# Chunked attention with a gated MLP on one core: two weight-sum sets a step from block 1, earlier splits at block changes, and P2 ahead of P7 in each first group

## The chip, the core and the metric

The kernel runs on one core of a Trainium2 chip. The core has five instruction queues that run side by side and meet at semaphores: TensorE (PE in the profile; its weight loads, PEld, overlap with its matmuls), VectorE (DVE), ScalarE (ACT), GpSimd (POOL) and SyncE (SP), which here issues all the transfers between memory and the on-chip buffers. Each queue runs its instructions in order, so an instruction that waits holds everything behind it on its own queue. The metric is device microseconds of one execution; three runs of the kernel before gave a median of 950.69 us (950.37 to 951.47).

## The reference, cut to what matters

```python
# q, k, v: (8, 8, 576, 64); attention inside chunks of 64
scores = scale * matmul(q_c, k_c.T); attn = softmax(scores); out = matmul(attn, v_c)
x = out.transpose(0, 2, 1, 3).reshape(4608, 512)
# w_gate, w_val: (512, 1536), w_out: (1536, 512)
gate = 1 / (1 + exp(-(x @ w_gate)));  val = x @ w_val
return (gate * val) @ w_out
```

All of it is float32. The kernel keeps the accuracy by splitting each operand into a high and a low part and adding three products (high by high, low by high, high by low) instead of one.

## The kernel before, in words

The 4608 tokens are nine blocks of 512 (m or n counts them), and the hidden width of 1536 is twelve tiles of 128 (f). Blocks 0 to 2 are computed plainly. A step of such a block is `hidden(m, f)`: 24 matmuls (L261) into two banks g0 (gate) and g1 (value), a sigmoid on ScalarE, a product on VectorE (`hf`, L272), and the split into `hh` and `hl`; then `down` (L287): 12 matmuls that add this tile's share to four accumulators `acc`. `down` runs one step behind `hidden`. After the last tile of a block four output copies (`evacuate`, L305 on ScalarE and L307 on VectorE, two each) empty the accumulators into tiles `ob`, and SP sends them out (L308).

Blocks 3 to 8 are computed as three pairs with a seven-product scheme in place of eight block products. P1 to P7 are `product(n, p, which, r, ...)` at L421: for each of 12 groups (p of six, gate or value), `first` computes P1 into bank x (`cx`) and P6 into y (`cy`), with `s1` and `u2` (L439) taken off them; `middle` computes P5 into z (`cz`), P7 on top of y and P2 on top of x; `last` computes P4 and P3. Then the output products (`outward`, L496) run for the pair's two blocks b = 0 and 1, twelve tiles each, every tile after a `split` into `hh` (ScalarE, L486) and `hl` (VectorE, L488).

The seven products need sums of weight quarters. There are 24 sets of them, and `keep_sums` (L331 to L349) computes one: two sums into a tile `a_val`, four into `a_sum`, then a high and a low part into `a_both`, all on GpSimd, and a transfer of `a_both` to memory by SP (L348). `a_val` and `a_sum` share the two buffers of the tag "ob" with the output copies' `ob` tiles of blocks 0 and 1 (and the first two of block 2), handed out in turn in the order of the program. `a_both` has one buffer. `keep(n)` emits the next n sets; it stands at the end of each step of blocks 1 and 2. GpSimd does nothing else in these blocks and runs through its sets as fast as buffers and `a_both`'s transfers let it, not in step with TensorE. In blocks 1 and 2 the order of TensorE and of VectorE is the program's, written out by hand; SP's order is set when the kernel is built, and is fixed then.

Beside the blocks runs the attention of later blocks, in units of two: SP loads `qt` and `kbd` (L149, L152) for scores, and `vt` (L158) for values; TensorE computes scores `sc` (L170) and values `av` (L231); VectorE does the softmax and its transposes (L520 to L560). `tick(share)` hands out VectorE's part of this work in small pieces at the places where it is called, and `insert` puts `sc` and `av` between other matmuls. `load_group` (L365, L368) brings given quarters and sums of a group back from memory into the buffers of weight tiles that are done with.

Of the kernel before, what the change touches and what calls it, by code (L numbers as in the profile page):

```python
# [19 lines left out]
NF = 12  # L20
# [24 lines left out]
SHARES = {1: 2.5, 2: 2.8, "up": 1.05, "down": 1.3}  # L45
# [3 lines left out]
def chunk_attn_moe(ctx: ExitStack, tc: tile.TileContext, q, k, v, w, out):  # L49
# [270 lines left out]
    def keep_given(p, which):  # L320

        t = given[p, which] = dp.tile([P, 3, 2, 256], F32, name=f"given{p}{which}")
        for n, (f, k) in enumerate(((2 * p, 0), (2 * p, 1), (2 * p + 1, 1))):
            nc.sync.dma_start(t[:, n], wt[f, which][:, :, k * 256:(k + 1) * 256].bitcast(F32))
# [6 lines left out]
    def keep_sums(p, which, c):  # L331

        if c == 0:
            sums[p, which] = dp.tile([P, 4, 2, 256], F32, name=f"sums{p}{which}")
        val = mp.tile([P, 4, P], F32, tag="ob", name="a_val")
        for n in range(2):
            parts = wt[2 * p + n, which].rearrange("p a (k c n) -> p a k c n", k=2, c=2)[:, :, :, c].bitcast(F32)
            nc.gpsimd.tensor_tensor(out=val[:, 2 * n:2 * n + 2], in0=parts[:, 0], in1=parts[:, 1], op=ALU.add)  # L338
        sm4 = mp.tile([P, 4, P], F32, tag="ob", name="a_sum")
        for o, x, y, op in (  # L340
            (sm4[:, 1], val[:, 2], val[:, 3], ALU.add), (sm4[:, 0], sm4[:, 1], val[:, 0], ALU.subtract),
            (sm4[:, 2], val[:, 0], val[:, 2], ALU.subtract), (sm4[:, 3], val[:, 1], sm4[:, 0], ALU.subtract),
        ):
            nc.gpsimd.tensor_tensor(out=o, in0=x, in1=y, op=op)  # L344
        both = wp.tile([P, 4, 2, P], F32R, tag="spare", name="a_both")
        nc.gpsimd.tensor_copy(both[:, :, 0], sm4)  # L346
        nc.gpsimd.tensor_tensor(out=both[:, :, 1], in0=sm4, in1=both[:, :, 0].bitcast(F32), op=ALU.subtract)  # L347
        nc.sync.dma_start(  # L348
            sums[p, which][:, :, c], both.rearrange("p s a n -> p s (a n)").bitcast(F32))  # L349
# [66 lines left out]
    def product(n, p, which, r, bank, start, stop):  # L416
        lhs, name = groups[n, p, which][r]
        x, k = xc[n, name], 0
        for c in range(2):
            for wpart, part in ((0, 0), (0, 1), (1, 0)):  # L420
                nc.tensor.matmul(  # L421
                    bank, lhsT=lhs(wpart, c), rhs=x[:, part, c], start=start and k == 0, stop=stop and k == 5,
                    skip_group_check=True)
                k += 1

    def sole(n, p, which):
        z = ps_g.tile([P, TB], F32, tag=f"g{which}", name="cz", bufs=1)
        product(n, p, which, 5, z, True, True)
        return z
# [12 lines left out]
    def gated(n, f, b, value):  # L442

        h = hid[n, f][:, b]
        nc.vector.tensor_tensor(out=h, in0=value, in1=h, op=ALU.mult)

    def middle(n, p, which):
        x, y, s1, u2 = banks[n, p, which]
        f = 2 * p
        if which == 0:  # L450
            for i in range(2):
                hid[n, f + i] = wp.tile([P, 2, TB], F32, tag=f"o{f + i}", name="hid")
        z = banks.pop((n, "z"), None) or sole(n, p, which)
        product(n, p, which, 7, y, False, True)
        u3 = mp.tile([P, TB], F32, tag="ob", name="u3")
        nc.vector.tensor_tensor(out=u3, in0=y, in1=s1, op=ALU.add)  # L456
        c22 = hid[n, f + 1][:, 1] if which == 0 else u3
        nc.vector.tensor_tensor(out=c22, in0=z, in1=u3, op=ALU.add)
        product(n, p, which, 2, x, False, True)
        if which == 0:  # L460
            nc.scalar.activation(hid[n, f][:, 0], x, AF.Sigmoid)
        else:
            gated(n, f + 1, 1, u3)
            gated(n, f, 0, x)
        banks[n, p, which] = y, z, s1, u2
# [17 lines left out]
    def split(n, f, b):  # L483
        h = hid[n, f][:, b]
        hh = mp.tile([P, TB], F32R, name="hh")
        nc.scalar.copy(hh, h)  # L486
        hl = mp.tile([P, TB], F32R, name="hl")
        nc.vector.tensor_tensor(out=hl, in0=h, in1=hh.bitcast(F32), op=ALU.subtract)  # L488
        return hh, hl
# [75 lines left out]
    def advance():  # L565
        now["unit"] += 2 * (now["item"] == "A")
        now["item"] = next(ahead, None)
        now["since"] = now["ticks"]

    def tick(share):  # L570
        now["ticks"] += 1
        now["credit"] += share
        while now["item"] is not None:
            if isinstance(now["item"], float):
                if now["credit"] < now["item"] / 2:
                    return
                now["credit"] -= now["item"]
            elif not (now["item"] == "wait" and now["ticks"] > now["since"] + 1
                      or now["item"][0] == "open" and now["item"][1] <= now["open"]):
                break  # L580
            advance()
        now["credit"] = min(now["credit"], share)
# [19 lines left out]
    def finish():  # L602
        down(*pending.pop(0))
# [30 lines left out]
    def keep(n):  # L634
        for _ in range(n):
            if kept:
                p, which, c = kept.pop(0)
                if c == 0:
                    keep_given(p, which)
                keep_sums(p, which, c)  # L640

    def rest():
        for m in range(1, FIRST_PAIR):
            upto = 4 * (m + 2) if m == 1 else 4 * (m + 3)
            for f in range(2 if m == 1 else 0, NF):
                if m == 2 and f == 7:
                    now["open"] = 0
                step(m, f, "")
                tick(SHARES[m])
                insert(upto, 2)  # L650
                finish()
                tick(SHARES[m])
                insert(upto, 2)
                if m == 1:
                    keep_outer(f)
                    if f == 11:
                        keep_outer(0), keep_outer(1)
                    keep(1)
                else:
                    keep(2)  # L660
                    if f == 8:
                        for which in range(2):
                            load_group(0, 0, which)
        for n in range(3):
            m0 = FIRST_PAIR + 2 * n
            upto = 4 * (m0 + 4)
            order = [(p, which) for p in range(6) for which in range(2)]
            due(n)
            for i, (p, which) in enumerate(order):
                if i + 1 < len(order) and i > 0:  # L670
                    load_group(n, *order[i + 1])
                if pending:
                    banks[n, "z"] = sole(n, p, which)
                    while pending:
                        finish()
                first(n, p, which)
                tick(SHARES["up"])
                if i:
                    last(n, *order[i - 1])
                    tick(SHARES["up"] if i < 11 else 0)  # L680
                    insert(upto, 1)
                middle(n, p, which)
                tick(SHARES["up"] if i < 11 else 0)
                insert(upto, 1)
            load_outer(0), load_outer(1)
            parts = split(n, 0, 0)
            last(n, *order[-1])
            now["open"] = n + 1
            for b in range(2):
                for f in range(NF):  # L690
                    if f % 2 == 0:
                        later = 6 * b + f // 2 + 2
                        if later < 12:
                            load_outer(later % 6)
                        elif n + 1 < 3:
                            load_group(n + 1, 0, later - 12)
                    hh, hl = parts if (b, f) == (0, 0) else split(n, f, b)
                    tick(SHARES["down"])
                    if (n, b) == (2, 1) and f >= NF - 2:
                        pending.append((f, hh, hl))  # L700
                        continue
                    for t in range(4):
                        outward(m0 + b, f, t, hh, hl)
                    insert(upto, 1)

        for i, tiles in ((0, (0, 1, 2)), (1, (0,)), (0, (3,)), (1, (1, 2, 3))):
            f, hh, hl = pending[i]
            for t in tiles:
                outward(NB - 1, f, t, hh, hl)
# [34 lines left out]
```

## Time and profile before

| | |
|---|---|
| median of three runs | 950.69 us (950.37 to 951.47) |
| the profiled execution: its own time, and its span | 949.0 us, 947.2 us |
| TensorE busy | 927.4 us, 98% of the span |
| VectorE, ScalarE, GpSimd busy | 601.1, 340.5, 139.0 us |
| GpSimd's 24 sets | 149.4 to 209.2 us (ten) and 265.1 to 353.1 us (fourteen) |
| block 1's output copies | 259.0 to 263.4 us |
| first group of the seven-product part | from 364.6 us |

The span is from the first to the last instruction; some 2 us of a run lie around it. A row of the timeline has the start in us, the duration in us (several instructions merged where it says x2 or more), engine, line, operation and tiles, and in brackets how long the engine had stood idle before it and what released it. A row of the waits has who waited for whom, the time in total, the number of times and the longest, in us. "SPq" is a transfer being issued.

### The profile page before, as it was taken

To read this page: it belongs to the slowest core of one execution; us is meant where nothing else is said; L and a number is where in the kernel's file an instruction comes from. 1 tells how busy PE (TensorE), PEld (TensorE's weight loads), DVE (VectorE), ACT (ScalarE), POOL (GpSimd) and SP (SyncE) were. 2 spreads that over 40 slices of the span, in tenths; PEclk is the share of its full clock that TensorE was granted. 3 is DMA by queue.
4 is the path that set the end of the run, shared out by engine and by line. 5 is a ranking of instruction groups with operands and counts; after the bars stand their busy time and mean duration, and the time that the engine had idled before them with its cause. 6 is when DMAs were issued, how large, how long until landed. Compare 5 with 4: busy or idle time off the path is not lost.

```text
span 947.2 us, 13080 instructions
## 1 busy us (share of the span) xinstructions
PE 927.4 (98%) x4960; PEld 762.0 (80%) x4960; DVE 601.1 (63%) x999; ACT 340.5 (36%) x556; POOL 139.0 (15%) x204
## 2 busy tenths in 40 slices
PE   6999999999999999999999999999999999999998
PEld 4778888888888887888887888888878888888886
DVE  6899973576576656766766666767686334445332
ACT  6899752233233242233142522232324221121222
POOL 1000006970079880000000000000000000000000
PEclk7999999999999999999999999999999999999999
DMA  8699894442243448657675756665565565556561
GB/s 290 210 305 298 313 305 168 134 145 78 64 137 112 134 141 312 203 200 229 205 246 207 254 186 219 211 220 201 190 222 197 193 208 183 203 184 215 218 222 45
DMA packets 81279, 189.61 MB, mean 200 GB/s; under 512 B 7488, under 2 KB 38208, under 8 KB 76608
## 3 DMA queue, kind: packets, MB, share of 16 engines
q1 hardware_dynamic: 81216, 188.77, 59.5%
q8 instruction: 39, 0.64, 0.3%
q14 instruction: 24, 0.20, 0.1%
HBM read 150.99 MB, written 37.75 MB: 199 GB/s over the span
## 4 chain that ended last, share of the span: by engine, by line
PE 81%; POOL 6%; DMA 6%; ACT 3%; DVE 2%; issue 1%; SPq 1%; POOLq 0%; ACTq 0%; DVEq 0%
PE acc L496 20%; PE cy L421 16%; PE g L261 13%; PE cz L421 11%; PE cx L421 10%; PE acc L287 6%; DMA sums<-a_both 3%; PE sc L170 3%; PE av L231 3%; POOL a_both L347 2%; POOL a_sum L344 2%; POOL a_both L346 1%; POOL a_val L338 1%; DMA out<-ob 1%; DMA wr<-sums 1%
## 5 line engine op out<-in xcount | busy, mean ns | idle before, releaser
L261 PE MATMUL g<-xt,w 128*128 128x512 f32 (+1 forms) x960 | 207.5, 371 | 3.0 <-ACT xt L249 1.3
L261 PEld LDWEIGHTS g<-xt,w 128*128 128x128 f32 x960 | 168.5, 189 | 36.3 <-ACT xt L249 1.7
L496 PE MATMUL acc<-wr,hh 128*128 128x512 f32 x576 | 177.8, 390 | 0.0
L421 PE MATMUL cy<-xc,wr 128*128 128x512 f32 x648 | 159.2, 389 | 0.9 <-DVE u L439 0.9
L421 PEld LDWEIGHTS cy<-xc,wr 128*128 128x128 f32 x648 | 121.5, 188 | 26.5 <-DVE u L439 1.3
L496 PEld LDWEIGHTS acc<-wr,hh 128*128 128x128 f32 x576 | 107.9, 188 | 22.7 <-ACT raw L242 0.3
L496 PE MATMUL acc<-wr,hl 128*128 128x512 f32 x288 | 112.7, 391 | 2.7 <-DVE hl L488 2.7
L421 PE MATMUL cz<-xc,wr 128*128 128x512 f32 x432 | 106.1, 391 | 1.1 <-DMA wr<-sums 1.1
L421 PE MATMUL cx<-xc,wr 128*128 128x512 f32 x432 | 106.0, 391 | 0.0
L560 DVE STREAM_TRANSPOSE pbd<-pr 32x256 f32<-32x256 f32 x224 | 97.6, 436 | 4.0
L488 DVE TENSOR_TENSOR hl<-hid,hh 128x512 fp32r<-128x512 f32 x72 | 49.5, 688 | 78.8 <-ACT hh L486 78.5
L421 PEld LDWEIGHTS cz<-xc,wr 128*128 128x128 f32 x432 | 80.5, 188 | 19.0 <-issue 2.5
L421 PEld LDWEIGHTS cx<-xc,wr 128*128 128x128 f32 x432 | 80.6, 188 | 17.5 <-issue 1.0
L287 PE MATMUL acc<-w,hh 128*128 128x512 f32 x288 | 90.4, 395 | 1.0 <-ACT hh L274 1.0
L486 ACT CAST hh<-hid 128x512 fp32r<-128x512 f32 x72 | 44.8, 622 | 127.1 <-PE acc L496 103.7
L338 POOL TENSOR_TENSOR a_val<-w 128x256 f32<-128x256 f32 x48 | 37.3, 798 | 202.2 <-ACT xt L249 144.7
L496 PEld LDWEIGHTS acc<-wr,hl 128*128 128x128 f32 x288 | 54.0, 188 | 16.0 <-DVE hl L488 4.8
L439 DVE TENSOR_TENSOR u<-cy,s 128x512 f32<-128x512 f32 x36 | 24.8, 688 | 63.3 <-PE cy L421 61.3
L272 DVE TENSOR_TENSOR hf<-g,hf 128x512 f32<-128x512 f32 (+1 forms) x40 | 25.4, 635 | 60.6 <-PE g L261 59.6
L287 PEld LDWEIGHTS acc<-w,hh 128*128 128x128 f32 x288 | 52.7, 188 | 13.1 <-issue 1.9
L456 DVE TENSOR_TENSOR u<-cy,s 128x512 f32<-128x512 f32 x36 | 24.9, 691 | 50.7 <-PE cy L421 50.5
L287 PE MATMUL acc<-w,hl 128*128 128x512 f32 x144 | 56.1, 389 | 0.0
(103 smaller groups left out, 1009.4 us busy)
## 6 DMA issues: line engine op xcount, KB each, us to landing
wr<-sums SPq DMA_DIRECT2D x72, 512.0 KB, 4.6
wr<-outer SPq DMA_DIRECT2D x36, 1024.0 KB, 4.9
w_raw<-w_in SPq DMA_DIRECT2D x36, 512.0 KB, 5.0
wr<-given SPq DMA_DIRECT2D x36, 512.0 KB, 3.7
sums<-a_both SPq DMA_DIRECT2D x24, 512.0 KB, 3.5
qt<-q_in SPq DMA_DIRECT2D x36, 256.0 KB, 4.4
kbd<-k_in SPq DMA_DIRECT2D x72, 128.0 KB, 4.4
vt<-v_in SPq DMA_DIRECT2D x36, 256.0 KB, 4.0
```

What stands on the lines that cost most here:

```text
L170: nc.tensor.matmul(sc[c * D:(c + 1) * D, (2 * a + t) * P:(2 * a + t + 1) * P], lhsT=s["qt"][:, a, n0:n0 + D], rhs=s["kb"][:, a, :, n0:n0 + D],
L231: nc.tensor.matmul(av[a * D:(a + 1) * D, c * P:(c + 1) * P], lhsT=s["vt"][:, a, c, :], rhs=pb[:, 4 * a + c, :, :], start=True, stop=True,)
L261: nc.tensor.matmul(ps[:, tok], lhsT=wt[f, which][:, wpart, c:c + P], rhs=x[:, part, i, tok], start=n == 0, stop=n == 11)
L272: nc.vector.tensor_tensor(out=hf, in0=pv, in1=hf, op=ALU.mult)
L287: nc.tensor.matmul(acc[m, t], lhsT=hx[:, ts], rhs=wt[f, 2][:, wpart], start=f == 0 and i == 0, stop=f == NF - 1 and i == 2,)
L338: nc.gpsimd.tensor_tensor(out=val[:, 2 * n:2 * n + 2], in0=parts[:, 0], in1=parts[:, 1], op=ALU.add)
L421: nc.tensor.matmul(bank, lhsT=lhs(wpart, c), rhs=x[:, part, c], start=start and k == 0, stop=stop and k == 5, skip_group_check=True)
L456: nc.vector.tensor_tensor(out=u3, in0=y, in1=s1, op=ALU.add)
L486: nc.scalar.copy(hh, h)
L488: nc.vector.tensor_tensor(out=hl, in0=h, in1=hh.bitcast(F32), op=ALU.subtract)
L496: nc.tensor.matmul(acc[m, t], lhsT=hx[:, ts], rhs=wo[f][:, wpart], start=f == 0 and i == 0, stop=f == NF - 1 and i == 2)
L560: nc.vector.transpose(out=pb[dst, :, c, h, i, :], in_=ps[src, h::2, k, :])
```

## The change

There are three edits. `keep(2)` now stands at the end of the steps of block 1 too, where `keep(1)` stood; so 20 sets, not 10, are emitted ahead of block 1's output copies, which come in the first step of block 2, and four sets follow in block 2 where fourteen did. In the first group of each pair (p = 0, gate) P2 runs ahead of P7. And at each pair, the first tile of block b = 1 is split as soon as the last tile of b = 0 has been split, ahead of the output copies of b = 0, with the `tick` at the very first tile left out.

```diff
@@ middle(n, p, which)
         z = banks.pop((n, "z"), None) or sole(n, p, which)
+        if (p, which) == (0, 0):
+            product(n, p, which, 2, x, False, True)
         product(n, p, which, 7, y, False, True)
         u3 = mp.tile([P, TB], F32, tag="ob", name="u3")
         nc.vector.tensor_tensor(out=u3, in0=y, in1=s1, op=ALU.add)
         c22 = hid[n, f + 1][:, 1] if which == 0 else u3
         nc.vector.tensor_tensor(out=c22, in0=z, in1=u3, op=ALU.add)
-        product(n, p, which, 2, x, False, True)
+        if (p, which) != (0, 0):
+            product(n, p, which, 2, x, False, True)
@@ rest(), steps of blocks 1 and 2
                     if f == 11:
                         keep_outer(0), keep_outer(1)
-                    keep(1)
-                else:
-                    keep(2)
+                keep(2)
+                if m == 2:
                     if f == 8:
                         for which in range(2):
                             load_group(0, 0, which)
@@ rest(), output products of a pair
-                    hh, hl = parts if (b, f) == (0, 0) else split(n, f, b)
-                    tick(SHARES["down"])
+                    hh, hl = parts if f == 0 else split(n, f, b)
+                    if (b, f) != (0, 0):
+                        tick(SHARES["down"])
+                    if (b, f) == (0, NF - 1):
+                        parts = split(n, 0, 1)
```

SP's queue around block 1's output copies (`out<-ob`), before: loads of scores and of values stand alone, and the next sums' transfer comes behind the copies.

```order
L158 DMA vt<-v_in 128x512 x2
L149 DMA qt<-q_in 128x512
L152 DMA kbd_87<-k_in 64x2x256 x2
L149 DMA qt<-q_in 128x512
L152 DMA kbd_88<-k_in 64x2x256 x2
L158 DMA vt<-v_in 128x512 x2
L308 DMA out<-ob 128x512 x4
```

The same place of SP's queue in the change:

```order
L158 DMA vt<-v_in 128x512 x2
L348 DMA sums_2537<-a_both 512x1x256
L348 DMA sums_2627<-a_both 512x1x256 x2
L149 DMA qt<-q_in 128x512
L152 DMA kbd_87<-k_in 64x2x256 x2
L149 DMA qt<-q_in 128x512
L152 DMA kbd_88<-k_in 64x2x256 x2
L158 DMA vt<-v_in 128x512 x2
L308 DMA out<-ob 128x512 x4
```

The transfers of sets 18, 19 and 20 now stand ahead of the scores' loads, the values' loads and the four outputs.

TensorE's first group of a pair, before (the last row also holds the start of the next group):

```order
L421 MATMUL cx<-xc,wr 128x512 x6
L421 MATMUL cy<-xc,wr 128x512 x12
L421 MATMUL cx<-xc,wr 128x512 x12
L421 MATMUL cy<-xc,wr 128x512 x12
L421 MATMUL cz<-xc,wr 128x512 x12
```

And in the change:

```order
L421 MATMUL cx<-xc,wr 128x512 x6
L421 MATMUL cy<-xc,wr 128x512 x6
L421 MATMUL cx<-xc,wr 128x512 x6
L421 MATMUL cy<-xc,wr 128x512 x6
L421 MATMUL cx<-xc,wr 128x512 x6
L421 MATMUL cy<-xc,wr 128x512 x12
L421 MATMUL cz<-xc,wr 128x512 x12
```

Six matmuls into x (P2) now lie between P6 and P7, both of which write y.

VectorE at the change from b = 0 to b = 1 of the first pair, before (`hl` is a split's second half, L307 the output copies):

```order
L488 TENSOR_TENSOR hl<-hid,hh 128x512 x2
L411 TENSOR_TENSOR xc<-raw,xc 128x1024
L400 TENSOR_TENSOR raw<-raw 128x2x512
L307 COPY ob<-acc 128x512
L307 COPY obs<-acc 128x512
L488 TENSOR_TENSOR hl<-hid,hh 128x512
```

And in the change (its lines behind the first edit are numbered three higher):

```order
L491 TENSOR_TENSOR hl<-hid,hh 128x512 x2
L307 COPY ob<-acc 128x512
L307 COPY obs<-acc 128x512
L411 TENSOR_TENSOR xc<-raw,xc 128x1024
L400 TENSOR_TENSOR raw<-raw 128x2x512
L491 TENSOR_TENSOR hl<-hid,hh 128x512
```

One more split stands ahead of the copies (the second of the first row is b = 1's first tile), and the two attention operations (L411, L400), which stood ahead of them, now stand behind.

## The prediction

> **What bounds the kernel now.** I read the page's busy times first, then TensorE's waits, then GpSimd's timeline, since the change is mostly about GpSimd's sums.
>
> ```profile
> PE 927.4 (98%) x4960; PEld 762.0 (80%) x4960; DVE 601.1 (63%) x999; ACT 340.5 (36%) x556; POOL 139.0 (15%) x204
> PE 81%; POOL 6%; DMA 6%; ACT 3%; DVE 2%; issue 1%; SPq 1%; POOLq 0%; ACTq 0%; DVEq 0%
> PE acc L496 <- DVE hl L488: 2.7, 5, 1.0
> PE cz L421 <- DMA wr<-sums: 1.1, 1, 1.1
> PE cy L421 <- DVE u L439: 0.9, 1, 0.9
> ```
>
> TensorE is busy 98% of the span. The chain of waits gives GpSimd and its transfers 12%, which looks like 100 us to win, but the chain only says that these ended last before one wait: TensorE worked on beside them. TensorE's own waits say what all three edits can win: the first product P5 waits 1.1 us for sums, P7 0.9 us for u2, and output products wait 2.7 us for `hl` in five places. That is 4.7 us, and whatever holds TensorE anywhere else is a full loss, because its order is fixed and it has nothing to make good with.
>
> **Edit 1, two sets a step in block 1.** GpSimd's first ten sets and the last fourteen (first and last instruction of each run):
>
> ```profile
> POOL 1000006970079880000000000000000000000000
> 149.37 1.44 POOL L338 TENSOR_TENSOR a_val<-w 128x256 f32<-128x256 f32 x2 [144.68 <-ACT xt L249]
> 207.91 1.28 POOL L347 TENSOR_TENSOR a_both<-a_sum,a_both 128x512 fp32r<-128x512 f32 x1
> 265.13 1.94 POOL L338 TENSOR_TENSOR a_val<-w 128x256 f32<-128x256 f32 x2 [55.94 <-DMA out<-ob]
> 350.95 2.15 POOL L347 TENSOR_TENSOR a_both<-a_sum,a_both 128x512 fp32r<-128x512 f32 x1
> 184.25 0.61 POOL L346 CAST a_both<-a_sum 128x512 fp32r<-128x512 f32 x1 [0.36 <-DMA sums<-a_both]
> 189.60 0.61 POOL L346 CAST a_both<-a_sum 128x512 fp32r<-128x512 f32 x1
> ```
>
> Ten sets take 149.37 to 209.19, 5.98 us a set; fourteen take 265.13 to 353.10, 6.28 us a set; a quick one, from cast to cast, 5.35. Between lie 55.94 us of idleness: set 11 needs "ob" buffers, which block 1's output copies use next. The change fills that gap with sets 11 to 20, and so turns the order round: now the copies need the buffers of set 20. Around the copies stands, before:
>
> ```profile
> 258.99 0.69 DVE L307 COPY ob<-acc 128x512 f32<-128x512 f32 x1 [0.70 <-PE acc L287]
> 262.22 0.69 DVE L307 COPY ob<-acc 128x512 f32<-128x512 f32 x1 [2.53 <-DMA out<-ob]
> 268.98 0.69 DVE L272 TENSOR_TENSOR hf<-g,hf 128x512 f32<-128x512 f32 x1
> 262.85 0.58 ACT L305 COPY ob<-acc 128x512 f32<-128x512 f32 x1 [2.59 <-DMA out<-ob]
> 259.71 4.08 SPq L308 DMA_DIRECT2D out<-ob  x4
> 266.32 1.97 PE L170 MATMUL sc<-kbd,qt 128*64 128x128 f32 x32
> 271.07 5.60 PE L261 MATMUL g<-xt,w 128*128 128x512 f32 x24
> 221.95 5.44 PE g L261 x24
> 247.95 2.72 PE acc L287 x12
> ```
>
> The last two rows are from the chain of waits and give TensorE's pace: 24 of these matmuls in 5.44 us, 12 in 2.72.
>
> The first copy is wanted at 258.99. Twenty sets at 5.98 us would end at 149.37 + 119.6 = 269.0. From 259 on VectorE stands still, and for the last 1.7 sets I take the quick set: 259 + 1.7 x 5.35 = 268.0. Now the queues behind it. SP's order puts set 20's transfer, then four score loads, two value loads, and then the first output:
>
> ```profile
> 197.43 0.51 SPq L348 DMA_DIRECT2D sums<-a_both  x1
> 198.03 0.58 SPq L149 DMA_DIRECT2D qt<-q_in  x1
> 200.98 1.43 SPq L152 DMA_DIRECT2D kbd<-k_in  x2
> 209.88 1.57 SPq L158 DMA_DIRECT2D vt<-v_in  x2
> DMA to landing us min/median/max: 2.5/4.4/7.0
> ```
>
> The sums' transfer takes 0.6 us to issue (268.6), the score loads 198.03 to 202.41, 4.4 us (273.0), the value loads 1.6 us (274.6). Two chains then reach TensorE.
>
> By VectorE: the third copy needs the first output's transfer, 2.5 us after its issue as before (259.71 to 262.22), so 277.1; VectorE's queue behind it (a reduction, the normalizing, seven transposes) brings `hf` 6.76 us later, as 262.22 to 268.98: it ends at 283.9 + 0.7 = 284.6 and frees bank g1. The 12 matmuls into g1 began at 271.07 + 2.72 (half of the 24) = 273.8 and begin at 284.65: 10.9 us late.
>
> By SP and TensorE: the last `kbd` is issued at 272.3 and lands 4.4 us later (the row of landings is that of `kbd`), 276.7. The scores, which began at 266.32, end at 277.7, not 268.2; 12 `down` matmuls (2.72) and 12 into g0 (2.72) bring TensorE to 283.1. So VectorE's chain ends last, by 1.5 us, but either alone costs 9 to 11 us. The cover is the 24 matmuls of the next step, which need neither chain and were started at 260.79; they are used up at 266.3.
>
> Two earlier loads are late too (one of score loads behind set 14, one of value loads behind set 17), by under 2 us each; they move nothing, since the stall is counted from GpSimd's own time.
>
> After a stall the clock has to be reckoned with:
>
> ```profile
> 8.00:12.00 4.00, 1.15 (x16) 0.94 (x12) 2.53 (x7) 2.92 (x17) 0.00 (x0) 0.77 1.02 392
> 12.00:16.00 4.00, 3.11 (x21) 2.40 (x21) 3.37 (x8) 3.90 (x9) 0.00 (x0) 0.50 1.10 300
> 11.51 1.08 PE L215 MATMUL tp<-ident,early 128*128 128x128 f32 x4 [2.85 <-DVE early L209]
> ```
>
> In the span's start TensorE waited 2.85 us, and over the next 4 us its granted clock (third number from the end) was 0.50. If the first 4 us of work after 277 run at half, they lose 2 us; 1.5 of these lie under VectorE's chain. I take 0.5; ends 0 and 2. The Trainium skill, "TensorE: Matmul & The Clock Gate", section "Part 1: The HAM clock gate (the "warmup" mystery)", has the clock halved after about 3.4 us without work and given back after as much work; by it the loss would be an estimated 1.7 us before the cover, so 0.2. The trace agrees with its half rate (0.50), though after a shorter wait.
>
> Edit 1's loss is 10.9 + 0.5 = 11.4 us. Ends: at 5.35 us a set GpSimd is done at 256.4, and nothing is lost; at 6.28 it is done at 275.0, 7.0 us later than taken, and 18 are.
>
> Its gain is at the other end of block 2:
>
> ```profile
> 353.12 0.52 SPq L348 DMA_DIRECT2D sums<-a_both  x1
> 357.74 0.43 SPq L368 DMA_DIRECT2D wr<-sums  x1
> 364.55 0.47 PE L421 MATMUL cz<-xc,wr 128*128 128x512 f32 x1 [1.12 <-DMA wr<-sums]
> 372.48 0.50 PE L421 MATMUL cy<-xc,wr 128*128 128x512 f32 x1 [0.85 <-DVE u L439]
> ```
>
> Set 24's transfer held SP until 353.1, the group's sums were asked for at 357.74, and P5 waited 1.12 us. In the change four sets are left for block 2; started some 16 us later than 265, they are done by about 281 + 4 x 6.28 = 306, far ahead. The wait goes: 1.1 us.
>
> **Edit 2, P2 ahead of P7.** P7 writes the bank that u2 is read from, and waited 0.85 us; six matmuls of P2 (1.4 us at the pace of 12 in 2.72) cover it. P2 needs P1's copy s1, two products old, and quarters that come in the first load. Gain 0.85 us in the first pair; the other pairs show no wait there, and gain nothing.
>
> **Edit 3, the earlier split.**
>
> ```profile
> 499.81 0.50 PE L496 MATMUL acc<-wr,hl 128*128 128x512 f32 x1 [0.98 <-DVE hl L488]
> 534.54 0.50 PE L496 MATMUL acc<-wr,hl 128*128 128x512 f32 x1 [0.25 <-DVE hl L488]
> 730.77 0.49 PE L496 MATMUL acc<-wr,hl 128*128 128x512 f32 x1 [0.25 <-DVE hl L488]
> 910.85 0.49 PE L496 MATMUL acc<-wr,hl 128*128 128x512 f32 x1 [0.25 <-DVE hl L488]
> ```
>
> The three changes from b = 0 to b = 1 wait 0.25 us each for the split that stood behind copies: 0.75 gained. The waits of 0.98 at a pair's second tile hang on ScalarE's cast, and lose 0.2 to 0.3 with one tick less ahead of them; I take 0.3 in all. The dropped tick shifts scores and values by a tile or so; they stay between the same products, and I count 0, ends -1 and +1.
>
> **Sum.** Lost 11.4; gained 1.1 + 0.85 + 0.75 + 0.3 = 3.0. Net +8.4 us on a profiled execution of 949.0 with a span of 947.2: span 955.6, execution 957.4. The median of the runs is 1.7 above that execution, so 959.1; I say 959.
>
> **The rivals.** (a) *GpSimd keeps up.* If its sets 11 to 20 run at 5.4 us, it is done before the first copy is wanted, and only the gains remain: 950.7 - 3.0 = 947.7. For it: the quick set, and that copies of weights to memory are mostly done by 150. Against it: ten sets in this very block took 5.98 with everything included, and fourteen 6.28. It decides below 5.5 us a set. The Trainium skill, "GPSIMD Engine Reference", section "1. Specifications", has GpSimd share its interfaces to the on-chip memory with VectorE, and slowed by VectorE's operations with two inputs there. By that rule the pace can't come down to 5.35 while VectorE works; the trace has 5.35 to 6.28, and no run here separates the cause.
>
> (b) *Half a stall.* At about 5.6 us a set GpSimd is done at 261.4, and the loss is 261.4 - 268.0 + 10.9 = 4.3, with the first edge of the clock none: +1.3, 952, within what a measurement can tell from no change (0.2%, 1.9 us, about the limit for this kernel).
>
> (c) *A longer stall.* At 6.28 us a set, with the clock's 2 us uncovered, 17.9 + 2 - 3.0 = +16.9: 967.6. For it: the fourteen sets' pace. Against it: that pace includes the slow last set beside VectorE's operand work (349 to 353), which block 1 does not have.
>
> (d) *The edit does not do what it says*: GpSimd's sets stay bound to block 2's steps, and edit 1 wins and loses nothing: 950.7 - 1.9 = 948.8. The order speaks against it: the transfers of sets 11 to 20 stand ahead of the copies.
>
> **How the numbers follow.** The forecast 0.70 (954 to 965), (a) 0.08, (b) 0.10, (c) 0.10, (d) 0.02. The likeliest time is 959. The range, 951.5 to 966, leaves out (a), (d) and the far half of (c). Slower by over 0.2% (over 952.6): the forecast, (c) and half of (b), 0.85. Within 0.2%: the other half of (b) and half of (d), 0.06. Faster: (a) and the rest of (d), 0.09.
>
> **What would show it.** In the changed kernel's timeline GpSimd works without a gap from 149 to about 268, the first VectorE copy L307 of block 1 starts at 267 to 269 with a wait for GpSimd, TensorE's scores wait for `kbd` from 267 on, and g matmuls that began at 271 begin near 282 to 285. TensorE's waits list some 10 us for `kbd` and `hf` that are not there now, and no wait of P5 for sums, of P7 for u2, and of `hl` at a change of blocks. It is wrong if GpSimd's twentieth set is done by 259, or if TensorE's g matmuls there start within 3 us of 271.

## The result and the profile after

The changed kernel takes 957.5 us (median of six runs, 956.5 to 960.2), the kernel before beside it 950.2 us (six runs, 949.4 to 951.5). The ratio is 1.0085, with a 95% interval from 1.0068 to 1.0102: slower, by 6.5 to 9.7 us. The profiled execution is the slowest of the six (960.18 us, span 958.4), so its times lie some 2.7 us above the median; its GpSimd starts its first set at 152.05 where the one before started at 149.37. Below, 2.7 us is taken off wherever a time of this trace is held against one of before. One kernel of the experiments (the sums issued by GpSimd, without block 1's output) has one slow execution, the profiled one (3286 us, its matmuls at about a third of their speed), so its other three are used and nothing is read from its trace.

The page's busy times, its GpSimd slices, and TensorE's waits, after:

```profile
PE 929.6 (97%) x4960; PEld 763.5 (80%) x4960; DVE 601.8 (63%) x999; ACT 340.7 (36%) x556; POOL 134.1 (14%) x204
POOL 1000006999838000000000000000000000000000
PE sc L170 <- DMA kbd<-k_in: 10.8, 4, 8.1
PE g L261 <- DVE hf L272: 1.3, 1, 1.3
PE cy L421 <- DVE u L458: 0.4, 1, 0.4
```

The busy times are nearly those of before (TensorE's grew by 2.2 us); what grew most is waiting, and one wait of 8.1 us for `kbd` is most of that. The waits of before for sums (1.1), for u2 (0.9) and for `hl` (2.7) are gone, and a wait of 0.4 for another u stands where P7's did. GpSimd's slices have no gap now: the sets run on into the time of block 1's output copies. The timeline there, GpSimd, VectorE and SP first, then TensorE:

```profile
152.05 1.45 POOL L338 TENSOR_TENSOR a_val<-w 128x256 f32<-128x256 f32 x2 [147.36 <-ACT xt L249]
267.25 0.69 DVE L307 COPY ob<-acc 128x512 f32<-128x512 f32 x1 [5.70 <-POOL a_sum L344]
269.31 1.26 POOL L347 TENSOR_TENSOR a_both<-a_sum,a_both 128x512 fp32r<-128x512 f32 x1
271.20 0.58 SPq L149 DMA_DIRECT2D qt<-q_in  x1
276.53 0.86 SPq L308 DMA_DIRECT2D out<-ob  x2
282.55 0.69 DVE L307 COPY ob<-acc 128x512 f32<-128x512 f32 x1 [14.62 <-DMA out<-ob]
289.31 0.69 DVE L272 TENSOR_TENSOR hf<-g,hf 128x512 f32<-128x512 f32 x1
...
277.19 1.97 PE L170 MATMUL sc<-kbd,qt 128*64 128x128 f32 x16 [8.10 <-DMA kbd<-k_in]
285.72 3.03 PE L261 MATMUL g<-xt,w 128*128 128x512 f32 x12 [0.76 <-ACT hf L270]
290.06 2.14 PE L261 MATMUL g<-xt,w 128*128 128x512 f32 x8 [1.30 <-DVE hf L272]
```

Set 20 ends at 270.57. The first copy waits 5.70 us for the buffer of set 20's `a_val`, which GpSimd (L344) had just read for the last time. That wait by itself costs nothing here: the copy is done at 267.94, but its output is issued only at 276.53, because SP's loads start when set 20's transfer has been issued, and the output stands behind them. From there it takes 6.0 us to the third copy, and 6.76 us more to `hf`. The second row of these matmuls is into g1; it begins at 290.06, 287.4 without the late start, where they began at 273.8: 13.6 us late.

TensorE's clock over this (windows of 4 us; the third number from the end is the granted clock, then the DMA engines' share and GB/s):

```profile
272.00:276.00 4.00, 0.00 (x0) 0.00 (x0) 0.00 (x0) 0.00 (x0) 0.00 (x0) 0.78 0.94 268
276.00:280.00 4.00, 2.47 (x22) 2.13 (x24) 0.00 (x0) 0.00 (x0) 0.00 (x0) 0.50 0.85 229
```

**Where the time went, by stage.** The starts of the first matmul of each stage, in us of each profile, give the lengths below; the four kernels on the right are experiments that follow. The second row is a part of the first: from the values `av` (L231) ahead of block 1's output copies to the next values.

| stage | before | the change | edit 1 alone | edits 2 and 3 | edit 3 alone | tick alone |
|---|---|---|---|---|---|---|
| scores at 130 to the first pair's P5 | 234.2 | 246.8 | 245.0 | 232.2 | 235.2 | 232.5 |
| of these, values at 256 to the next values | 28.72 | 42.87 | 41.10 | 28.72 | 28.72 | 28.72 |
| first pair, P5 to output products | 130.94 | 130.36 | 130.83 | 130.36 | 130.95 | 130.83 |
| first pair's output products | 71.41 | 69.52 | 71.34 | 69.53 | 69.52 | 69.52 |
| second pair's products | 126.96 | 126.96 | 126.96 | 126.95 | 126.96 | 126.96 |
| second pair's output products | 69.25 | 67.40 | 69.26 | 67.40 | 67.40 | 67.95 |
| third pair's products | 114.24 | 114.24 | 114.24 | 114.24 | 114.24 | 114.24 |
| third pair's output products, to the last matmul | 65.61 | 65.05 | 65.64 | 65.06 | 65.05 | 65.60 |

The change loses 12.6 us ahead of P5 and wins 4.9 behind it. The stages behind P5 agree to 0.1 us between kernels that share an edit; the first stage differs by 3.0 us between kernels without a stall (232.2 to 235.2), so a us there means little. Its part around the copies does not differ between them (28.72 us), and so it is the best measure of the stall: 14.1 us in the profile of the change, and 12.4 in that of edit 1 alone, where set 20 ended 1.2 us earlier against TensorE's work.

### The profile page after: what moved, and what is told of

Read it like the earlier page. It is cut to its first block, busy times and chain, and to the rows that moved or that the text cites. A ratio compares the mean times of both kernels' runs of the same rounds, so it can differ in the third digit from the quotient of the medians.

```text
span 958.4 us, 13077 instructions
## 1 busy us (share of the span) xinstructions
PE 929.6 (97%) x4960; PEld 763.5 (80%) x4960; DVE 601.8 (63%) x999; ACT 340.7 (36%) x556; POOL 134.1 (14%) x204
## 4 chain that ended last, share of the span: by engine, by line
PE 70%; POOL 9%; DMA 8%; DVE 5%; ACT 4%; issue 2%; SPq 1%; ACTq 0%; DVEq 0%; POOLq 0%
PE acc L499 21%; PE cy L421 15%; PE cz L421 10%; PE cx L421 10%; PE g L261 6%; PE acc L287 4%; DMA w_raw<-w_in 3%; POOL a_sum L344 3%; POOL a_both L347 3%; DMA sums<-a_both 2%; POOL a_val L338 2%; PE sc L170 2%; PE av L231 2%; POOL a_both L346 1%; DMA out<-ob 1%
## 5 line engine op out<-in xcount | busy, mean ns | idle before, releaser
L499 PEld LDWEIGHTS acc<-wr,hl 128*128 128x128 f32 x288 | 54.1, 188 | 11.3
```

The source lines that it names most:

```text
L499: nc.tensor.matmul(acc[m, t], lhsT=hx[:, ts], rhs=wo[f][:, wpart], start=f == 0 and i == 0, stop=f == NF - 1 and i == 2)
```

## The experiments

The theory: twenty sets end after the copies want their buffers, and two chains from there hold TensorE: score loads behind set 20's transfer on SP, and the output copies on VectorE. The rivals tested are that the loss comes from GpSimd's work itself, that one chain is the whole of it, and that the gains are elsewhere than predicted.

**How many sets ahead?** Edits 2 and 3 alone (ten sets ahead of the copies), and the change with sixteen and with eighteen; each has one of the three new lines below in place of the change's, in this order. The fourth kernel is the one before with edit 1 alone (twenty sets):

```diff
-                keep(2)
+                keep(1 if m == 1 else 2)
+                keep(1 if m == 1 and f >= 8 else 2)
+                keep(1 if m == 1 and f >= 10 else 2)
```

> The change with one set a step in block 1 again (edits 2 and 3 alone). If the loss is the stall at block 1's output copies, made by edit 1, this run has no such stall and keeps the gains of edits 2 and 3, predicted at 1.9 us: 948.3 us, ratio about 0.998. Rival: the loss comes from the moved attention pieces (the dropped tick) or from P2's new place; then this run stays near 957.

> Two sets a step in block 1 alone, without edits 2 and 3. If edit 1 makes the loss: 957.5 + 1.9 = 959.4 us, with TensorE waiting 8 to 11 us for the scores' kbd near 270 and for hf near 290 as in the changed kernel. If edits 2 and 3 make a part of the loss, it lies below 957.

> The change with 16 sets ahead of block 1's copies (two a step, one in the last four), 8 left for block 2. At the 5.9 us a set of the changed kernel's profile GpSimd is done 95 us after it starts (about 245), 14 us before the copies: no stall. The eight left are done by about 265 + 8 x 6.3 = 315, so P5's wait for sums is gone too. All three gains: 950.2 - 3.0 = 947.2 us, ratio 0.997. Rival: that any sets above ten in block 1 cost by traffic or by slowing VectorE; then this run lies halfway, near 953.

> 18 sets ahead of the copies. At 5.93 us a set GpSimd is done 106.7 us after its start, about 256, some 3 us before the first copy: the copies themselves don't wait. By the theory of the stall (a threshold near 18 sets) this is 947 to 950 us, the value loads behind set 17 being the only late thing; by a cost that grows with each set above ten it is near 955.

Measured: ten sets 944.6 us, ratio 0.9952 [0.9930, 0.9974]; sixteen 944.8, 0.9953 [0.9937, 0.9969]; eighteen 944.5, 0.9954 [0.9937, 0.9971]; edit 1 alone 961.2, 1.0121 [1.0091, 1.0151]. Between eighteen sets and the twenty of the change lie (1.0085 - 0.9954) x 950 = 12.4 us: the loss is a threshold, not a price per set. What GpSimd does beside block 1 costs nothing up to sixteen sets, where the stage around the copies takes 28.72 us as with ten. With eighteen it takes 30.76, so a stall of 2.0 us has begun, too small for the times to tell. Two things were not as expected: edits 2 and 3 win 4.6 us, not 2, and sixteen or eighteen sets win nothing on top of ten.

The kernel with eighteen sets stands at the edge:

```profile
256.17 1.29 POOL L347 TENSOR_TENSOR a_both<-a_sum,a_both 128x512 fp32r<-128x512 f32 x1
260.94 0.69 DVE L307 COPY ob<-acc 128x512 f32<-128x512 f32 x1 [0.71 <-PE acc L287]
263.37 7.88 SPq L308 DMA_DIRECT2D out<-ob  x4
268.26 1.97 PE L170 MATMUL sc<-kbd,qt 128*64 128x128 f32 x32
269.70 0.69 DVE L307 COPY ob<-acc 128x512 f32<-128x512 f32 x1 [8.07 <-DMA out<-ob]
276.46 0.69 DVE L272 TENSOR_TENSOR hf<-g,hf 128x512 f32<-128x512 f32 x1
277.21 3.02 PE L261 MATMUL g<-xt,w 128*128 128x512 f32 x12 [1.29 <-DVE hf L272]
```

The copy is on time and the scores do not wait, yet the third copy is held 8.07 us: the output was issued at 263.37, behind the loads, and landed 6.3 us later, and TensorE waits 1.29 us for `hf`. With ten sets it goes out ahead of the score loads, behind two value loads only:

```profile
259.53 4.02 SPq L308 DMA_DIRECT2D out<-ob  x4
261.97 0.69 DVE L307 COPY ob<-acc 128x512 f32<-128x512 f32 x1 [2.47 <-DMA out<-ob]
268.73 0.69 DVE L272 TENSOR_TENSOR hf<-g,hf 128x512 f32<-128x512 f32 x1
```

There it is 2.4 us. The third copy is 6.76 us ahead of `hf` in both, as predicted; the output's landing is what differs.

**Is it the copies or the loads?** Block 1's output is left out of the change, so that nothing waits for set 20's buffers:

```diff
     def evacuate(m, t, last=False):
+        if m == 1:
+            if t % 2:
+                nc.scalar.copy(warm, acc[m, t][:, :1])
+            else:
+                nc.vector.tensor_copy(warm, acc[m, t][:, :1])
+            return
```

> The change, where block 1's four accumulators are read (one column each, into a tile of one column) but no output tile is made and its rows are not sent: block 1's output is left out. So neither VectorE nor ScalarE waits for set 20's buffers or for an output transfer; the score loads stay behind set 20's transfer in SP's queue. If the loads alone hold TensorE by 9 to 11 us, this run is 955 to 957 us, with the wait for kbd as long as in the changed kernel and none for hf. If the copies' chain makes the loss, it is near 947.

Measured: 954.8 us, ratio 1.0063 [1.0042, 1.0084].

```profile
PE sc L170 <- DMA kbd<-k_in: 10.8, 4, 8.3
257.95 13.72 SPq L354 DMA_DIRECT2D sums<-a_both  x3
277.07 3.68 PE L170 MATMUL sc<-kbd,qt 128*64 128x128 f32 x32 [8.33 <-DMA kbd<-k_in]
```

SP stands in three transfers of sums for 13.72 us, and the score loads are issued behind them; the wait for `hf` is gone. So the loads alone cost (1.0063 - 0.9953) x 950 = 10.4 us against kernels without a stall, as the prediction had it ("either alone costs 9 to 11"). The stage around the copies has 11.1 (39.84 us): the wait of 8.33, and 2.7 that the scores and the `down` behind them take longer at the halved clock (3.61 and 3.85 us where they took 1.90 and 2.85 before).

**The loads taken off SP's queue.** Score and value loads of the units concerned are issued by ScalarE; once with block 1's output, once without it (the value loads' line is changed like the first):

```diff
-        nc.sync.dma_start(qt, q[g, u].rearrange("p (a n) -> p a n", a=2))
+        queue = nc.scalar if 10 <= j < 20 else nc.sync
+        queue.dma_start(qt, q[g, u].rearrange("p (a n) -> p a n", a=2))
...
-            nc.sync.dma_start(kb[s, :, i, :], k[g, u, s].rearrange("p (a n) -> p a n", a=2))
+            queue.dma_start(kb[s, :, i, :], k[g, u, s].rearrange("p (a n) -> p a n", a=2))
```

> The change with the score and value loads of the five attention pairs in blocks 1 and 2 issued by ScalarE instead of SP, so they don't stand behind the sums' transfers. The copies still wait for set 20's buffers and the third one for the first output. If the copies' chain alone costs nearly as much as both: the third copy about 3 us after set 20 (no loads between them), hf 6.8 us later, a loss of 4 to 6 us where the changed kernel has 13, so about 951 us. If only the loads count, near 947; if only the copies count with their full wait, near 957.

> Both of the two changes before: loads from ScalarE's queue, and block 1's output copies cut to a column and its output left out. All 20 sets stay in block 1. If these two chains make the whole stall, it is gone: 950.2 - 3.0 = 947.2 us, less up to 0.5 for the four copies and outputs left out. If 20 sets in block 1 cost by themselves (traffic, VectorE slowed, TensorE's operands read more slowly), it stays above 950.

Measured: 958.9 us, ratio 1.0099 [1.0062, 1.0137]; without the output 968.1, 1.0184 [1.0144, 1.0225]. The first lies near its third branch (957), but by luck: TensorE does not wait for `hf` on VectorE there, and waits 12.0 us for a sigmoid. The second misses. Only the wait for `kbd` went as meant; the second kernel's waits and ScalarE's timeline show what came instead:

```profile
PE g L263 <- ACT hf L272: 19.0, 6, 8.6
191.94 5.77 ACTq L153 DMA_DIRECT2D kbd<-k_in  x2
197.81 0.60 ACT L272 ACTIVATE hf<-g 128x512 f32<-128x512 f32 x1 [9.78 <-DMA sums<-a_both]
```

The sigmoid stands in ScalarE's queue behind the issuing of loads, and TensorE waits for the sigmoid. The row of 5.77 us is two issues of 0.54 to 1.03 us each and the time between them; the profile names a transfer of sums as what ended ScalarE's idle time, and why the loads waited for it is not shown. These two kernels replace the stall by another and say nothing on the theory.

**The sums taken off SP's queue.** Here GpSimd issues its sums' transfers itself, and the loads stay on SP; again with block 1's output and without it:

```diff
-        nc.sync.dma_start(
+        nc.gpsimd.dma_start(
             sums[p, which][:, :, c], both.rearrange("p s a n -> p s (a n)").bitcast(F32))
```

> The change, with the transfers of the sums issued by GpSimd itself instead of SP, so that the score and value loads no longer stand behind them in SP's queue. It leaves the chain through the output copies as it is. Theory (two chains, one by the copies and one by the loads, each late by itself): the wait for kbd goes, the third copy of block 1 waits only some 3 us for the first output since no load lands beside it, hf comes some 6.8 us after that copy, and 4 to 6 us of the stall are left: about 949 to 951, ratio 1.000 +/- 0.002. Rival (the loads alone are the stall): 945 to 946, ratio 0.9955. Rival (GpSimd's own issues cost it about 1 us a set, so its twentieth set ends some 20 us later): over 965.

> As the kernel with the sums' transfers issued by GpSimd, and block 1's output is left out: its accumulators are read by one-column copies and its rows are not sent, so nothing waits for the buffers of set 20 and nothing for its transfer. Theory (the two chains together are the whole stall): no wait for kbd or hf near 270 to 290, and the time of the kernel with one set a step in block 1, 944.5 to 946, ratio 0.9955. Rival (GpSimd's twenty sets in block 1 cost time in some other way, by the on-chip memory or by the engines that they run beside): a ratio of 1.000 or more, with waits spread over block 1.

Measured with the output: 962.7 us, ratio 1.0142 [1.0123, 1.0161].

```profile
PE acc L287 <- DVE ob L307: 13.2, 1, 13.2
152.09 1.30 POOL L347 TENSOR_TENSOR a_both<-a_sum,a_both 128x512 fp32r<-128x512 f32 x1
277.10 0.73 POOL L348 DMA_DIRECT2D sums<-a_both  x1 [0.40 <-POOL a_both L347]
279.69 0.69 DVE L307 COPY ob<-acc 128x512 f32<-128x512 f32 x1 [22.12 <-POOL a_sum L344]
281.24 1.26 POOL L347 TENSOR_TENSOR a_both<-a_sum,a_both 128x512 fp32r<-128x512 f32 x1
282.54 0.69 DVE L307 COPY ob<-acc 128x512 f32<-128x512 f32 x1 [2.16 <-DMA out<-ob]
282.53 0.59 ACT L305 COPY ob<-acc 128x512 f32<-128x512 f32 x1 [24.98 <-POOL a_both L347]
287.90 5.74 PE L261 MATMUL g<-xt,w 128*128 128x512 f32 x24 [0.49 <-ACT hf L270]
```

The second rival's cause came true, though not its size (set 20 some 20 us later, over 965 us): each transfer costs GpSimd 1.1 us (0.40 of waiting and 0.73 of issuing), nineteen sets take 281.24 - 152.09 = 129.2 us, 6.8 a set where the change has 5.9, and set 20 ends at 282.5, not 270.6. The scores are on time, and with no load beside it the output lands 2.2 us after the copy; but the copies come 12 us later than in the change, and then even the accumulators' banks are not free for the next `down` (13.2 us). So waiting for set 20's buffers is enough for a stall, longer or shorter with the end of set 20. Its length at the change's own pace, with SP's queue free of the sums, has not been measured. An estimate: here ScalarE's first copy, at 282.53 when set 20 had ended, is 5.37 us ahead of the matmuls into g0 (287.90); in the change set 20 ends at 267.9 without the late start, so these would begin at 273.3 where they began at 271.07, and some 2 us of the stall would be left. Most of it would then hang on the order of SP's queue.

Without the output: 942.7 us, ratio 0.9923 [0.9907, 0.9939], from three executions and without a trace to read. There is no loss: with both chains gone the stall is gone, and GpSimd's work costs nothing that the times show in another way. Against the kernel with only the copies' chain gone, the loads' chain is (1.0063 - 0.9923) x 950 = 13.3 us, some 2.5 either way by the two intervals.

**A control that was none.** Ten sets ahead, without block 1's output, was to say what leaving out the output is worth by itself (the output is left out as above):

```diff
-                keep(2)
+                keep(1 if m == 1 else 2)
```

> Control for the kernels that leave out block 1's output: one set of sums a step in block 1 (edits 2 and 3 only), and block 1's output left out in the same way (its accumulators read by one-column copies, its rows not sent). There is no stall here to take away. Theory (in the kernel whose sums GpSimd sends, without block 1's output, both chains and with them the whole stall are gone): the same ratio as there, 0.992 to 0.993. Rival (leaving out block 1's output is worth nothing by itself): 0.9952 as with the output, and the 0.9923 there is chance. If it is worth w, the score-load chain alone costs more than the 10.4 us that I worked out against 0.9953: (1.0063 - this ratio) x 950.

Measured: 954.9 us, ratio 1.0054 [1.0035, 1.0073], outside both expectations. The page's GpSimd slices, SP's queue and the scores:

```profile
POOL 1000006999991000000000000000000000000000
257.77 13.75 SPq L354 DMA_DIRECT2D sums<-a_both  x3
271.61 0.58 SPq L149 DMA_DIRECT2D qt<-q_in  x1
277.20 3.22 PE L170 MATMUL sc<-kbd,qt 128*64 128x128 f32 x27 [8.63 <-DMA kbd<-k_in]
```

Without the copies nothing makes set 11 wait for a buffer, so GpSimd does all 24 sets from 151 to 293 without a gap although the program emits one a step, SP's order has three transfers of sums ahead of the score loads, and the wait of 8.6 us for `kbd` is back. What leaving out the output is worth in the time of the whole kernel is therefore not known, and by the times 10.4 and 13.3 us for the loads' chain stand side by side. The stage around the copies decides for the lower: it takes 40.03 us here, 11.3 more than before, and 11.1 more in the kernel above whose loads alone are late. The loads' chain shows once more, with one set a step: what counts is which set's transfer stands ahead of the score loads, not how many the program emits.

**Where the gain comes from.** Edit 3 alone, and of it only the tick that is left out:

```diff
                     hh, hl = parts if (b, f) == (0, 0) else split(n, f, b)
-                    tick(SHARES["down"])
+                    if (b, f) != (0, 0):
+                        tick(SHARES["down"])
```

> Edit 3 alone: the first tiles of block 1 of a pair split ahead of the output copies, and no tick after a pair's first down tile; sums and the order of P2 and P7 as before. Predicted at first: 1.05 us gained, ratio 0.999. Theory now (what the profile of the change shows by stages: 1.9 us less in each of the first two pairs' output stages, 0.5 in the third's): 4.2 us gained, ratio 0.9956. The first pair's products up to its output stage take as long as before.

> Only the tick after a pair's first down tile is left out; block 1's first tiles are split where they were. Theory (the dropped tick lets VectorE do the second tile's hl ahead of a reduction): the waits of 0.98 at the second tile go in two pairs, the waits of 0.25 at the change of blocks stay; by the stages 1.3 to 1.5 us gained in each of the first two output stages, together 2.6 to 3, ratio 0.997. Rival (what I predicted: the waits hang on ScalarE's cast): 0.3 us, ratio 0.9997.

Measured: edit 3 alone 946.2 us, ratio 0.9956 [0.9938, 0.9975]; the tick alone 945.3, 0.9955 [0.9942, 0.9969]. The one tick gives all of the gain that the runs can measure. VectorE's rows at the first pair's second tile, before:

```profile
497.50 1.21 DVE L542 TENSOR_REDUCE sums<-pr 128x16 f32<-128x1024 f32 x1
499.13 0.63 DVE L488 TENSOR_TENSOR hl<-hid,hh 128x512 fp32r<-128x512 f32 x1
```

and with the tick left out (whole program some 1.5 us earlier there):

```profile
496.23 0.69 DVE L488 TENSOR_TENSOR hl<-hid,hh 128x512 fp32r<-128x512 f32 x1
496.84 1.21 DVE L542 TENSOR_REDUCE sums<-pr 128x16 f32<-128x1024 f32 x1
726.14 0.50 PE L496 MATMUL acc<-wr,hl 128*128 128x512 f32 x1 [0.25 <-DVE hl L488]
```

The tick had put a softmax reduction with its small operations ahead of the second tile's `hl`. The last row, of TensorE, is the second pair's change of blocks, where the wait of 0.25 stays as long as the first tile is split behind the copies. In the stage table the tick is worth 1.89 us in the first pair and 1.30 in the second, the earlier split 0.55 in each of the last two pairs. In the first pair the tick takes the wait at the change of blocks away as well.

## Why the prediction was right, step by step

The forecast was 959.0 us; 957.5 was measured, in the range and on the side that was given 0.85. Both the loss and the gains are larger than predicted, and their errors cancel in part; so the mechanism of the loss was right, and that the sum came so close is partly luck.

- **GpSimd's pace: right; the first copy: earlier than predicted.** Twenty sets from 152.05 to 270.57 are 5.93 us a set (5.98 was taken, with a quicker end). Set 20 was to end at 268.0, at 270.7 with the late start; it ended at 270.57. The first copy was put at set 20's end. It came at 267.25, 3.3 us ahead of that end, since it needs the buffer of `a_val` and not that of `a_sum`; without the late start that is 264.6, ahead of the 267 to 269 that were given. Nothing hangs on it, because the output waits for SP.
- **The loads' chain: right in mechanism and nearly in size.** The last `kbd` was to land at 276.7, 279.4 with the late start, and the second half of the scores, which needs it, began at 279.50 (the first half at 277.19). Their end was predicted at 277.7, 280.4 with the late start; `down` follows at 281.27, 0.9 later, because 16 of these matmuls took 1.77 us at the halved clock and not 1. Alone the chain costs 10.4 us by the nearest kernels (9 to 11 predicted), 13.3 by the other pair, and 11.1 and 11.3 by the stage around the copies.
- **The copies' chain: right in mechanism, mis-sized in one term.** "2.5 us after its issue as before" was taken from an output that stands behind two value loads only; behind the score and value loads it took 6.0. The third copy was predicted at 277.1 (279.8 with the late start) and came at 282.55; the 6.76 us to `hf` held to 0.01. So g1 was 13.6 us late, not 10.9. The landing was known to depend on its place in SP's queue, since the order showed it behind the loads; the row from which I took it stood ahead of the score loads. ScalarE's part of the chain, its second copy and the sigmoid behind it, was left out of the prediction; it held the matmuls into g0 by 0.76 us, and VectorE's `hf` ended later.
- **The clock: inside its bounds.** 0.5 us was taken, and in the change it costs nothing on top. The clock was at half in 276 to 280 while TensorE did the late scores, and what that cost lies under the wait for `hf` (1.30 us), which ended later. Where nothing covers it, in the kernel without block 1's output, the halved clock costs 2.7 us, more than the 2 of the upper bound. By the profile's windows of 1 us it fell at about 274.2, 5.1 us after TensorE's last matmul, and came back at 281.1, 3.9 us after the scores began. The Trainium skill, "TensorE: Matmul & The Clock Gate", section "Part 1: The HAM clock gate (the "warmup" mystery)", gives a free-running window of about 3.4 us for both: the trace agrees with that here (5.1 and 3.9 us, if a window began only after the pause or the work had), though the start of before fell to half inside a wait of 2.85 us.
- **Edit 1's gain of 1.1: not shown.** The wait of P5 for sums is not the program's but one execution's. It is 1.1 us in the profile of before, 1.9 with edit 3 alone, and absent with the tick alone and with edits 2 and 3, all of which have the sets where they were:

```profile
PE cz L421 <- DMA wr<-sums: 1.9, 1, 1.9
```

  (This row of TensorE's waits is of edit 3 alone.) Sixteen and eighteen sets, which take the cause of that wait away, are no faster than ten.
- **Edit 2: about 0.5 by the stages, 0.85 predicted.** The first pair's products take 130.36 us with it and 130.83 without it (130.94 where P5 also waited for sums). The wait of 0.85 for u2 went, and the next `cy` waits 0.4 for the next u. The gain is too small for the times to tell.
- **Edit 3: the step that was wrong.** 0.75 and 0.3, together 1.05, were predicted; the stages show 4.3, the times 4.2. Two errors made it: the waits of 0.98 at the second tile were put down to ScalarE's cast of `hh`, though TensorE's row named VectorE's `hl` and VectorE had been busy with a reduction. And a wait costs more than its row says. TensorE's rows around the first pair's two waits, before:

```profile
498.21 0.61 PE L496 MATMUL acc<-wr,hh 128*128 128x512 f32 x2
500.15 0.63 PE L496 MATMUL acc<-wr,hh 128*128 128x512 f32 x2
500.62 0.40 PE L496 MATMUL acc<-wr,hl 128*128 128x512 f32 x1
500.85 0.62 PE L496 MATMUL acc<-wr,hh 128*128 128x512 f32 x2
...
533.67 0.61 PE L496 MATMUL acc<-wr,hh 128*128 128x512 f32 x2
534.54 0.50 PE L496 MATMUL acc<-wr,hl 128*128 128x512 f32 x1 [0.25 <-DVE hl L488]
534.88 0.40 PE L496 MATMUL acc<-wr,hh 128*128 128x512 f32 x1
```

  Undisturbed, two `hh` matmuls and one `hl` take 0.47 + 0.23 from start to start. Around the wait of 0.25 it is 0.87 + 0.34, so 0.51 more; around the one of 0.98 (`hl` at 499.81) 1.60 + 0.34, so 1.24. Two of 1.24 and three of 0.51 make 4.0 of the 4.3.
- **The rivals.** "GpSimd keeps up" and "half a stall" fell with the pace; the quick set of 5.35 us ran while VectorE stood idle for 4.85 us (until 190.62). The lower end that went with it, sets done at 256.4 and nothing lost, is not borne out: in the kernel with eighteen sets the last one ends at 257.46, 255.5 against TensorE's work of before, and 2.0 us are lost, as the output still stands behind the loads; "a longer stall" was right only in that it is longer (g1 13.6 us late, between the 10.9 of the forecast and its 17.9), and for another reason (the output's landing, not GpSimd's pace); "the edit does not do what it says" is refuted by GpSimd's timeline.
- **The sum.** Lost 12.4 by the times and 14.1 by the stage around the copies (11.4 predicted, without the gain of 1.1), gained 4.3 to 4.6 (3.0 predicted): by the times +7.8 to +8.1 against +8.4.

The kernels that beat both are the ones without edit 1's last two sets: with ten, sixteen or eighteen sets they take 0.9952 to 0.9954 of the time before, and leaving out one tick alone does the same (0.9955).

## What to carry to other kernels

Work that is given to an idle engine costs nothing until its buffers or its transfers stand ahead of somebody else's on a queue that runs in order; so look for the last item of that work, in the order of each queue, and ask what is issued right behind it, since that sets a threshold and not a price per item. When an operation is taken from a profile to be placed elsewhere, take its duration from a row with the same neighbours in its queue (here the same output took 2.4 us ahead of the score loads and 6.0 to 6.3 behind them). And for a short wait read the row's releaser and what that engine did just before: one badly placed piece of unrelated work on an engine that runs in order can hold another (here a reduction on VectorE cost TensorE 1.24 us), and the starts of the waiter's instructions show the cost better than its idle time.

## What the runs showed of the hardware that was not expected

- **An output behind loads lands when the bytes ahead of it have moved.** From issue to the next copy it takes 2.4 us behind two value loads, and 6.0 and 6.3 us behind 1.5 MB of score and value loads (two `qt` of 256 KB, four `kbd` of 128 KB, two `vt` of 256 KB). In the change 2.1 MB stood ahead of it, with set 20's sums of 512 KB; from 271.1 to its issue at 276.53 the profile has 245 GB/s, so an estimated 1.3 MB had moved. The 0.8 MB left and the first two outputs (0.5 MB) at the 213 GB/s of the next 6.02 us are an estimated 6.1 us. The Trainium skill, "DMA: Bandwidth & Descriptors", section "Queues, rings and completion order", has the transfers that one engine issues share its rings, whose descriptors are consumed in order; the trace agrees.
- **A short wait of TensorE costs about 0.26 us more than its idle time** in this stream of 128x512 matmuls: 0.51 for 0.25, and 1.24 for 0.98.
- **Issuing transfers holds a computing engine.** One transfer of sums cost GpSimd 1.1 us a set, 0.9 us in its pace. ScalarE's queue stood 5.77 us at two `kbd` loads, whose issues take 0.54 to 1.03 us each.
- **Leaving work out moved other work.** Block 1's output, left out, let GpSimd run all 24 sets early and brought the stall back in a kernel that had none.
